# Splitting the first layer-norm tile into two column halves, and loading from two queues at the start of a gated linear-attention and token-MLP kernel

## The chip, the cores and the metric

The kernel runs on one core of a Trainium2 chip. The core has a matrix engine (TensorE, PE in the profile), a vector engine (VectorE, DVE), a scalar engine (ScalarE, ACT), a general engine (GpSimd, POOL) and a sync engine (SyncE, SP). Each works through its own list of instructions in order, and they meet through semaphores. Loads from device memory (DMA) can be issued by SP or by ACT; each of the two has a queue of its own (q1 and q10 in the profile), and the packets of both run on the core's 16 DMA engines. The metric is the device time of one execution in microseconds (us); lower is better.

## The reference, cut to what matters

```python
def _B_ref(x, w1, b1, w2, b2):
    h = _layernorm(x, axis=-1)                       # (x - mean) / sqrt(var + eps), per row of 512
    u = jnp.einsum("bsd,sf->bdf", h, w1) + b1        # contracts the 2048 tokens
    u = _gelu(u)
    y = jnp.einsum("bdf,fs->bds", u, w2) + b2
    return transpose(y)

g = _sigmoid((x * gate_w).sum(-1, keepdims=True))
a = _A_ref(x, wqkv, wo)                              # linear attention, 32 heads
out = g * a + (1 - g) * _B_ref(x, w1, b1, w2, b2)    # x: 1 x 2048 x 512, F = 1792
```

The change touches only the beginning of `_B_ref`: the layer norm of x, the first product with `w1`, and how the biases `b1` and `b2` get from rows to columns.

## The kernel before, in words

x has 2048 rows, held as 16 tiles of 128 partitions by 512 columns (`xr[:, t, :]`). F = 1792 is 14 blocks of 128 columns; the first 7 blocks (`NFA`) are half A, loaded as `w1A`, one load of 128 x 896 for each token tile t.

The start goes through these steps for each tile t. SP loads `xr` tile t and `w1A` tile t, in the order x 0, x 1, w 0, x 2, w 1, x 3, w 2, x 4, w 3 and so on. DVE takes the statistics (`ln_bn`, line 202; `ln_aggr`, line 205). ACT takes the square root (`ln_root`, line 209). DVE takes the reciprocal and writes the normalised tile `xh[:, t, :]` (`ln_apply`, lines 215 and 218). TensorE then multiplies: for tiles 0 to 11 it runs seven matmuls for each tile, one into each of seven PSUM banks `accA[j]` (`mlp1`, line 273, through the helper `mm`, so line 76 in the profile); the last four tiles (`TAIL`) are run bank by bank, with a GELU on ACT after each bank.

Two orders matter. First, DVE runs the statistics of tile t+1 before it applies tile t (line 230 before line 231), and DVE works in order. Second, nearly everything is pinned to the written order (`pin`, `keep_in_program_order`), so what stands first in the text stands first in its engine's list. In the built program each load also waits for an earlier one: eight completion semaphores are used in turn, so a load is issued only when the load eight before it has landed.

Ahead of the first real matmul TensorE runs 16 matmuls of 128 x 256 on constant data (`warm_ps`, lines 191 to 193) and one small matmul, `vps` (line 195): it turns the 30 rows `b_rows` (b1 as 14 rows and b2 as 16 rows of 128) into 30 columns. ACT copies these columns to `b1_sb` and `b2_sb` (lines 238 and 239) after the square root of tile 1. ACT issues the two small loads of `b_rows` as its first work, ahead of the load of its function table (line 140).

After half A the kernel goes on with the keys (`kacc`), the state (`Gps`), half B of the MLP (`accB`), the queries (`qacc`) and the second MLP product (`yps`), which ends it. None of these is edited.

Of the kernel before, what the change touches and what calls it, by code (L numbers as in the profile page):

```python
# [9 lines left out]
ALU = mybir.AluOpType  # L10
AX = mybir.AxisListType
BF16 = mybir.dt.bfloat16
FP32 = mybir.dt.float32
# [3 lines left out]
def kernel(  # L17
# [13 lines left out]
    nc = tc.nc  # L31
    P = nc.NUM_PARTITIONS
# [7 lines left out]
    S, D = X.shape  # L40
    F = B_w1.shape[1]
    NT = S // P
    ND = D // P
    NF = F // P
# [3 lines left out]
    NFA = NF // 2  # L48
    FA = NFA * P
    TAIL = 4  # L50

    x_view = X.rearrange("(t p) d -> p t d", p=P)
# [3 lines left out]
    w1_view = B_w1.rearrange("(t p) f -> p t f", p=P)  # L56
    w2_view = B_w2.rearrange("(f p) s -> p f s", p=P)
    b1_view = B_b1.rearrange("(f p) -> f p", p=P)
    b2_view = B_b2.rearrange("(t p) -> t p", p=P)
# [4 lines left out]
    work = ctx.enter_context(tc.tile_pool(name="work", bufs=3))  # L64
# [3 lines left out]
    def ptile(shape, dt, name):  # L68
        return persist.tile(shape, dt, name=name, tag=name)

    def bank(name):
        return psum.tile([P, SC], FP32, name=name, tag="bank")

    def mm(o, lhsT, rhs, start, stop, **kw):
        tc.keep_in_program_order(
            nc.tensor.matmul(o, lhsT=lhsT, rhs=rhs, start=start, stop=stop, **kw)  # L76
        )

    xr = ptile([P, NT, D], BF16, "xr")
    xh = ptile([P, NT, D], BF16, "xh")  # L80
# [13 lines left out]
    ident = ptile([P, P], BF16, "ident")  # L94
    gw_b = ptile([P, D], BF16, "gw_b")
    b_rows = ptile([NF + NT, P], BF16, "b_rows")
    b1_sb = ptile([P, NF], FP32, "b1_sb")
    b2_sb = ptile([P, NT], FP32, "b2_sb")
    mv = ptile([P, NT, nc.vector.BN_AGGR_DIM], FP32, "mv")
    sd = ptile([P, NT], FP32, "sd")  # L100
    rstd = ptile([P, NT], FP32, "rstd")
# [20 lines left out]
    w1A = wpool.tile([P, NT, FA], BF16, name="w1A", tag="w")  # L122
    w1B = wpool.tile([P, NT, FA], BF16, name="w1B", tag="w")

    pin = tc.keep_in_program_order

    def load(o, i, eng=None, **kw):
        pin((eng or nc.sync).dma_start(out=o, in_=i, **kw))

    def load_x(t0, t1):  # L130
        load(xr[:, t0:t1, :], x_view[:, t0:t1, :])

    def load_w1a(t):
        load(w1A[:, t, :], w1_view[:, t, 0:FA])


    tbl = work.tile([P, 1], FP32, name="tbl", tag="tbl", bufs=2)
    load(b_rows[0:NF, :], b1_view, nc.scalar)
    load(b_rows[NF : NF + NT, :], b2_view, nc.scalar)
    pin(nc.scalar.activation(out=tbl[:], in_=eps_t[:], func=ACT.Sqrt))  # L140

    load_x(0, 1)
    for t in range(5):
        load_x(t + 1, t + 2)
        load_w1a(t)
    load_w1a(5)
    for t0 in range(6, NT, 2):
        load_x(t0, t0 + 2)
        load_w1a(t0)
        load_w1a(t0 + 1)  # L150
# [9 lines left out]
    for t0 in range(0, NT, 4):  # L160
# [9 lines left out]
        out=mask[:], in_=mask[:], compare_op=ALU.is_gt, fill=1.0,  # L170
# [3 lines left out]
        out=mask[:], in_=mask[:], compare_op=ALU.is_ge, fill=0.0,  # L174
# [4 lines left out]
        out=maskH[:], in_=maskH[:], compare_op=ALU.is_gt, fill=1.0,  # L179
# [3 lines left out]
        out=maskH[:], in_=maskH[:], compare_op=ALU.is_ge, fill=0.0,  # L183
# [7 lines left out]
    warm_ps = bank("warm_ps")  # L191
    for _ in range(16):
        mm(warm_ps[:, :256], warm[:, 0:P], warm[:], True, True)
    vps = bank("vps")
    mm(vps[:, : NF + NT], b_rows[:], ident[0 : NF + NT, 0 : NF + NT], True, True)


    stats = {}

    def ln_bn(t):  # L200
        stats[t] = work.tile([P, nc.vector.BN_STATS_DIM], FP32, name="stats", tag="stats", bufs=4)
        pin(nc.vector.bn_stats(out=stats[t][:], in_=xr[:, t, :]))  # L202

    def ln_aggr(t):
        pin(nc.vector.bn_aggr(out=mv[:, t, :], in_=stats[t][:]))

    def ln_root(t0, t1):
        pin(
            nc.scalar.activation(
                out=sd[:, t0:t1], in_=mv[:, t0:t1, 1], func=ACT.Sqrt, bias=eps_t[:], scale=1.0  # L210
            )
        )

    def ln_apply(t0, t1):
        pin(nc.vector.reciprocal(out=rstd[:, t0:t1], in_=sd[:, t0:t1]))
        for t in range(t0, t1):
            pin(
                nc.vector.tensor_scalar(
                    out=xh[:, t, :], in0=xr[:, t, :],
                    scalar1=mv[:, t, 0:1], scalar2=rstd[:, t : t + 1],  # L220
                    op0=ALU.subtract, op1=ALU.mult,
                )
            )

    ln_groups = [(t, t + 1) for t in range(6)] + [(t, t + 2) for t in range(6, NT, 2)]
    ln_bn(0)
    ln_aggr(0)
    ln_root(0, 1)
    for (p0, p1), (t0, t1) in zip(ln_groups[:-1], ln_groups[1:]):
        ln_bn(t0)  # L230
        ln_apply(p0, p1)
        ln_aggr(t0)
        for t in range(t0 + 1, t1):
            ln_bn(t)
            ln_aggr(t)
        ln_root(t0, t1)
        if t0 == 1:
            pin(nc.scalar.copy(out=b1_sb[:], in_=vps[:, :NF]))
            pin(nc.scalar.copy(out=b2_sb[:], in_=vps[:, NF : NF + NT]))
    ln_apply(*ln_groups[-1])  # L240


# [26 lines left out]

    accA = [bank("accA") for _ in range(NFA)]  # L270

    def mlp1(acc, w, col, t, last):
        mm(acc[:], w[:, t, col : col + P], xh[:, t, :], t == 0, last)

    for t in range(NT - TAIL):
        for j in range(NFA):
            mlp1(accA[j], w1A, j * P, t, False)
    for j in range(NFA):
        for t in range(NT - TAIL, NT):
            mlp1(accA[j], w1A, j * P, t, t == NT - 1)  # L280
        gelu(accA[j], j)
# [59 lines left out]
    def mlp1_block(j):  # L341
        acc = bank("accB")
        for t in range(NT):
            mlp1(acc, w1B, (j - NFA) * P, t, t == NT - 1)
        return acc
# [76 lines left out]
    for b in range(NFA):  # L422
        acc = mlp1_block(NFA + b)
# [56 lines left out]
    for c in range(NSC):  # L480
        for j in range(ND):
# [5 lines left out]
                    out=pqT[:, j, c * SC : (c + 1) * SC],  # L487
                    in0=pqT[:, j, c * SC : (c + 1) * SC], in1=rex[:], op=ALU.mult,
# [55 lines left out]
```

## Time and profile before

| what | time |
|---|---|
| median of 3 runs | 165.81 us (165.55 to 165.82) |
| the profiled execution | 165.61 us |
| its span, first to last instruction | 163.9 us |
| TensorE busy in it | 158.7 us (97%) |
| DVE busy | 95.3 us (58%) |
| ACT busy | 52.1 us (32%) |
| first warming matmul | 1.25 us after the span's start |
| first `accA` matmul | 5.01 us after the span's start |

The span runs from the first to the last instruction, so the profiled execution has 1.7 us outside it. Lines of the timeline give the start, the time to the end of the group, the engine, the source line, the operation with its output and inputs, the count, and, in brackets, how long the engine stood idle before and what ended that. SPq and ACTq are the instructions with which SP and ACT issue loads. PEld is the load of a matmul's fixed operand. Lines of a table by windows give, for each stretch, the busy time and the instructions started on PE, PEld, DVE, ACT and POOL, the granted TensorE clock, the busy share of the DMA engines and what they moved in GB/s.

### The profile page before, as it was taken

The numbers are of one execution on the slowest core, as the hardware profiler recorded it, in microseconds if no ns is written. First come the engines' busy times: TensorE is split into PE (matmuls) and PEld (weight loads), VectorE is DVE, ScalarE is ACT, GpSimd is POOL, SyncE is SP. The second block draws the span as 40 slices with busy tenths as digits, with TensorE's granted clock in tenths as the row PEclk, the third lists the DMA queues.
The fourth block names the chain that finished last, engine by engine and source line by source line (L and its number), as shares of the span: only waits on it lengthen the run. The fifth ranks groups of instructions, "written<-read, shape, count | busy, mean of one in ns | idle before, by whom it ended". The sixth has DMA issues, their size and how long they took to land.

```text
span 163.9 us, 2114 instructions
## 1 busy us (share of the span) xinstructions
PE 158.7 (97%) x765; PEld 74.2 (45%) x779; DVE 95.3 (58%) x224; ACT 52.1 (32%) x87; POOL 2.0 (1%) x15
## 2 busy tenths in 40 slices
PE   6999999999999999999999999999999999999992
PEld 4444444444444455444444344444444444444461
DVE  3789989699989978482749743657205111111131
ACT  4221147952433214252348511007222221111110
POOL 4000000000000000000000000000000000000000
PEclk9999999999999999999999999999999999999999
DMA  4999996454999998000000003569982001101001
GB/s 122 293 361 374 365 147 141 101 109 86 366 384 359 367 386 305 4 4 0 2 0 0 4 32 125 187 199 301 388 322 84 32 34 48 46 32 36 32 32 32
DMA packets 26086, 25.57 MB, mean 156 GB/s; under 512 B 9820, under 2 KB 22492, under 8 KB 26076
## 3 DMA queue, kind: packets, MB, share of 16 engines
q1 hardware_dynamic: 26016, 25.43, 49.7%
q8 instruction: 6, 0.10, 0.2%
q14 instruction: 4, 0.03, 0.1%
q10 hardware_dynamic: 60, 0.01, 0.0%
HBM read 21.11 MB, written 2.23 MB: 142 GB/s over the span
## 4 chain that ended last, share of the span: by engine, by line
PE 97%; issue 1%; DVE 0%
PE yps L76 29%; PE accA L76 15%; PE accB L76 15%; PE kacc L76 8%; PE aps L76 8%; PE qacc L76 8%; PE Gps L76 8%; PE warm_ps L76 2%; PE denps L76 1%; PE kvps L76 1%; PE w2ps L76 1%; DVE ot L473 0%; DVE warm L118 0%; PE zcol_ps L76 0%; PE vps L76 0%
## 5 line engine op out<-in xcount | busy, mean ns | idle before, releaser
L76 PE MATMUL yps<-uT,w2h 128*128 128x512 bf16 (+1 forms) x234 | 50.1, 367 | 0.2
L76 PEld LDWEIGHTS <-w2h 128*128 128x128 bf16 x238 | 23.3, 98 | 25.3
L473 DVE SCALAR_TENSOR_TENSOR ot<-yps,c,ga 128x512 bf16<-128x512 f32 (+1 forms) x17 | 12.0, 717 | 36.6 <-PE yps L76 27.7
L464 ACT ACTIVATE ga<-aps,c,gg 128x512 f32<-128x512 f32 x16 | 12.4, 777 | 46.7 <-PE aps L76 46.3
L76 PE MATMUL accB<-xh,w1B 128*128 128x512 bf16 x110 | 25.1, 379 | 0.1
L76 PE MATMUL accA<-xh,w1A 128*128 128x512 bf16 x110 | 24.7, 385 | 0.1
L76 PEld LDWEIGHTS <-w1A 128*128 128x128 bf16 x112 | 11.0, 99 | 13.5 <-issue 0.8
L76 PEld LDWEIGHTS <-w1B 128*128 128x128 bf16 x112 | 10.9, 98 | 13.4 <-issue 0.4
L76 PE MATMUL kacc<-wk_sb,xT 128*128 128x512 bf16 x63 | 15.7, 379 | 0.1
L76 PE MATMUL aps<-W2sb,pqT 128*128 128x512 bf16 x63 | 15.6, 379 | 0.1
L76 PE MATMUL Gps<-pk,xr 128*128 128x512 bf16 x62 | 15.5, 379 | 0.1
L286 ACT ACTIVATE e<-qacc 128x512 bf16<-128x512 f32 x16 | 9.6, 597 | 16.1 <-PE qacc L76 15.3
L76 PE MATMUL qacc<-xT,wq_sb 128*128 128x512 bf16 x62 | 14.4, 379 | 0.1
L288 DVE TENSOR_SCALAR e<-e 128x512 bf16<-128x512 bf16 x32 | 9.2, 288 | 8.5 <-ACT e L286 8.2
L286 ACT ACTIVATE e<-kacc 128x512 bf16<-128x512 f32 x16 | 9.2, 598 | 12.7 <-DVE pk L293 6.8
L202 DVE BATCH_NORM_STATS2 stats<-xr 128x6 f32<-128x512 bf16 x16 | 10.7, 669 | 3.0 <-DMA xr<-in_A_x_dram 3.0
L293 DVE SCALAR_TENSOR_TENSOR pk<-kacc,e 128x512 bf16<-128x512 f32 x16 | 11.1, 692 | 1.0
L293 DVE SCALAR_TENSOR_TENSOR pqT<-qacc,e 128x512 bf16<-128x512 f32 x16 | 11.1, 691 | 0.6
L486 DVE TENSOR_TENSOR pqT<-pqT,rex 128x512 bf16<-128x512 bf16 x16 | 6.8, 426 | 6.1 <-DMA rex<-rd_dram 6.0
L250 DVE CUSTOM_DVE_ANT_0 junk<-xr,gw_b 128x512 bf16<-128x512 bf16 x16 | 9.9, 684 | 0.0
L76 PEld LDWEIGHTS <-xr 128*128 128x128 bf16 x64 | 6.2, 98 | 7.6
L76 PEld LDWEIGHTS <-pqT 128*128 128x128 bf16 x64 | 6.3, 98 | 7.6
(65 smaller groups left out, 80.2 us busy)
## 6 DMA issues: line engine op xcount, KB each, us to landing
w2h<-in_B_w_dram SPq DMA_DIRECT2D x4, 1792.0 KB
w1A<-in_B_w_dram SPq DMA_DIRECT2D x16, 224.0 KB
w1B<-in_B_w_dram SPq DMA_DIRECT2D x4, 896.0 KB
rex<-rd_dram SPq DMA_DIRECT2D x16, 128.0 KB
out_dram<-ot SPq DMA_DIRECT2D x15, 128.0 KB
xr<-in_A_x_dram SPq DMA_DIRECT2D x5, 256.0 KB
xr<-in_A_x_dram SPq DMA_DIRECT2D x6, 128.0 KB
wk_sb<-in_A_wqkv_dram SPq DMA_DIRECT2D x1, 512.0 KB
```

Source lines behind the costliest of these rows:

```text
L76: nc.tensor.matmul(o, lhsT=lhsT, rhs=rhs, start=start, stop=stop, **kw)
L202: pin(nc.vector.bn_stats(out=stats[t][:], in_=xr[:, t, :]))
L250: nc.vector.tensor_tensor_reduce(out=junk[:], in0=xr[:, t, :], in1=gw_b[:], scale=1.0, scalar=0.0, op0=ALU.mult, op1=ALU.add, accum_out=gp ...
L286: pin(nc.scalar.activation(out=e[:], in_=acc[:], func=ACT.Exp))
L288: nc.vector.tensor_scalar(out=e[:], in0=e[:], scalar1=1.0, scalar2=PHI_EPS, op0=ALU.min, op1=ALU.add)
L293: nc.vector.scalar_tensor_tensor(out=o, in0=acc[:], scalar=0.0, in1=e[:], op0=ALU.max, op1=ALU.add)
L464: nc.scalar.activation(out=ga[:], in_=aps[:], func=ACT.Identity, scale=gg[:, t : t + 1], bias=c2[:, t : t + 1])
L473: nc.vector.scalar_tensor_tensor(out=ot[:, d0:d1], in0=yps[:, d0:d1], scalar=c1[:, t : t + 1], in1=ga[:, d0:d1], op0=ALU.mult, op1=ALU.add,)
L486: nc.vector.tensor_tensor(out=pqT[:, j, c * SC : (c + 1) * SC], in0=pqT[:, j, c * SC : (c + 1) * SC], in1=rex[:], op=ALU.mult,)
```

## The change

Tile 0 of x is loaded as two halves of 256 columns, the first from SP and the second from ACT. ACT also loads `w1A` tiles 0 and 1, ahead of its function table. SP goes on with x 1, x 2, x 3 and `w1A` 2, then with the two small loads of `b_rows`, then with x 4, w 3, x 5, w 4, w 5 and the rest as before.

For tile 0, DVE takes statistics of each half (two `bn_stats` whose results one `bn_aggr` joins) and normalises each half by itself. TensorE multiplies the first half with all seven blocks and then the second half: 14 matmuls of 256 columns for the seven of 512. The `vps` matmul moves from before the tile 0 matmuls to behind them, and the two copies of its result on ACT move from behind the square root of tile 1 to behind all the square roots and the GELU table load.

```diff
+    HD = D // 2
+    load(xr[:, 0, 0:HD], x_view[:, 0, 0:HD])
+    load(xr[:, 0, HD:D], x_view[:, 0, HD:D], nc.scalar)
+    load_w1a(0, nc.scalar)
+    load_w1a(1, nc.scalar)
     tbl = work.tile([P, 1], FP32, name="tbl", tag="tbl", bufs=2)
-    load(b_rows[0:NF, :], b1_view, nc.scalar)
-    load(b_rows[NF : NF + NT, :], b2_view, nc.scalar)
     pin(nc.scalar.activation(out=tbl[:], in_=eps_t[:], func=ACT.Sqrt))
-
-    load_x(0, 1)
-    for t in range(5):
-        load_x(t + 1, t + 2)
-        load_w1a(t)
+    for t in range(1, 4):
+        load_x(t, t + 1)
+    load_w1a(2)
+    load(b_rows[0:NF, :], b1_view)
+    load(b_rows[NF : NF + NT, :], b2_view)
+    for t in range(4, 6):
+        load_x(t, t + 1)
+        load_w1a(t - 1)
     load_w1a(5)
...
-    vps = bank("vps")
-    mm(vps[:, : NF + NT], b_rows[:], ident[0 : NF + NT, 0 : NF + NT], True, True)
...
+    def parts(t):
+        return [(0, HD), (HD, D)] if t == 0 else [(0, D)]
+
     def ln_bn(t):
-        stats[t] = work.tile([P, nc.vector.BN_STATS_DIM], FP32, name="stats", tag="stats", bufs=4)
-        pin(nc.vector.bn_stats(out=stats[t][:], in_=xr[:, t, :]))
+        n = len(parts(t))
+        stats[t] = work.tile([P, n, nc.vector.BN_STATS_DIM], FP32, name="stats", tag="stats", bufs=4)
+        for i, (d0, d1) in enumerate(parts(t)):
+            pin(nc.vector.bn_stats(out=stats[t][:, i, :], in_=xr[:, t, d0:d1]))
...
         for t in range(t0, t1):
-            pin(
-                nc.vector.tensor_scalar(
-                    out=xh[:, t, :], in0=xr[:, t, :],
-                    scalar1=mv[:, t, 0:1], scalar2=rstd[:, t : t + 1],
-                    op0=ALU.subtract, op1=ALU.mult,
+            for d0, d1 in parts(t):
+                pin(
+                    nc.vector.tensor_scalar(
+                        out=xh[:, t, d0:d1], in0=xr[:, t, d0:d1],
+                        scalar1=mv[:, t, 0:1], scalar2=rstd[:, t : t + 1],
+                        op0=ALU.subtract, op1=ALU.mult,
+                    )
                 )
-            )
...
-        if t0 == 1:
-            pin(nc.scalar.copy(out=b1_sb[:], in_=vps[:, :NF]))
-            pin(nc.scalar.copy(out=b2_sb[:], in_=vps[:, NF : NF + NT]))
...
-    def mlp1(acc, w, col, t, last):
-        mm(acc[:], w[:, t, col : col + P], xh[:, t, :], t == 0, last)
+    def mlp1(acc, w, col, t, last, d0=0, d1=D):
+        mm(acc[:, d0:d1], w[:, t, col : col + P], xh[:, t, d0:d1], t == 0 and d0 == 0, last)
 
     for t in range(NT - TAIL):
-        for j in range(NFA):
-            mlp1(accA[j], w1A, j * P, t, False)
+        for d0, d1 in parts(t):
+            for j in range(NFA):
+                mlp1(accA[j], w1A, j * P, t, False, d0, d1)
+        if t == 0:
+            vps = bank("vps")
+            mm(vps[:, : NF + NT], b_rows[:], ident[0 : NF + NT, 0 : NF + NT], True, True)
+            pin(nc.scalar.copy(out=b1_sb[:], in_=vps[:, :NF]))
+            pin(nc.scalar.copy(out=b2_sb[:], in_=vps[:, NF : NF + NT]))
```

## The prediction

> **What bounds the kernel now.** I read the chain of waits first, then the timeline of the first 9 us, then the load queue of SP and the windows by microsecond.
>
> The chain of waits up to 13 us (start, length, what):
>
> ```profile
> 1.25 3.59 PE warm_ps L76 x16
> 4.85 0.13 PE vps L76
> 4.98 0.04 issue
> 5.01 7.59 PE accA L76 x32
> 12.60 0.05 issue
> ```
>
> From 1.25 us to the end it is TensorE without a real pause (97% of the span). So the time is when `accA` starts, plus its work, plus whatever idle time a change opens. Beyond the start there is nothing to win: 16 warming matmuls, a gap, and then a full engine.
>
> The timeline of that start:
>
> ```profile
> 2.97 0.69 DVE L202 BATCH_NORM_STATS2 stats<-xr 128x6 f32<-128x512 bf16 x1 [1.76 <-DMA xr<-in_A_x_dram]
> 3.69 0.18 DVE L205 BATCH_NORM_AGGREGATE mv<-stats 128x2 f32<-128x6 f32 x1
> 3.79 0.66 DVE L202 BATCH_NORM_STATS2 stats<-xr 128x6 f32<-128x512 bf16 x1
> 3.91 0.29 ACT L209 ACTIVATE sd<-mv,eps_t 128x1 f32<-128x1 f32 x1 [0.57 <-DVE mv L205]
> 4.37 0.14 DVE L215 RECIPROCAL rstd<-sd 128x1 f32<-128x1 f32 x1
> 4.55 0.41 DVE L218 TENSOR_SCALAR xh<-xr,mv,rstd 128x512 bf16<-128x512 bf16 x1
> 4.98 0.14 PEld L76 LDWEIGHTS <-w1A 128*128 128x128 bf16 x2
> 5.40 0.15 PEld L76 LDWEIGHTS <-w1A 128*128 128x128 bf16 x1 [0.28 <-issue]
> 5.82 0.15 PEld L76 LDWEIGHTS <-w1A 128*128 128x128 bf16 x1 [0.28 <-issue]
> 6.18 2.90 PEld L76 LDWEIGHTS <-w1A 128*128 128x128 bf16 x14 [0.21 <-issue]
> ```
>
> `xh` of tile 0 is ready at 4.55 + 0.41 = 4.96, and `accA` starts at 5.01. The weight loads come 0.42 us apart, and from 6.18 on 0.21 apart (14 in 2.90): until about 6.1 us the array runs at half its later rate, whatever the granted clock of 1.00 in the rows. The 16 warming matmuls show the same half rate: 256 columns every 0.21 us, so they stream until 1.25 + 16 x 0.213 = 4.66.
>
> Loads of SP, and the windows (PE, PEld, DVE, ACT, POOL, clock, DMA share, GB/s):
>
> ```profile
> 3.62 0.43 SPq L128 DMA_DIRECT2D w1A<-in_B_w_dram  x1
> 7.80 0.33 SPq L128 DMA_DIRECT2D w1A<-in_B_w_dram  x1
> ...
> 2.00:3.00 1.00, 1.00 (x7) 0.67 (x6) 0.03 (x1) 1.00 (x1) 0.64 (x5) 1.00 0.83 261
> 3.00:4.00 1.00, 1.00 (x6) 0.67 (x5) 0.97 (x3) 0.42 (x3) 0.00 (x0) 1.00 0.79 186
> 4.00:5.00 1.00, 0.98 (x5) 0.41 (x4) 0.96 (x4) 0.20 (x1) 0.00 (x0) 1.00 0.90 304
> ```
>
> Every load waits for the one eight before it. The issue at 7.80 (w 7) stands on w 2, which was issued at 3.62: SP was free 0.26 us earlier (7.21 + 0.33 = 7.54), so w 2 landed near 7.78. By then x 0 to x 3 and w 0 to w 2 had to be in, 4 x 131 + 3 x 229 = 1,212 KB. The row of 3 to 4 us shows a dip, 186 against 304 GB/s.
>
> **The change part by part.**
>
> *Start of tile 0.* A half of `bn_stats` isn't in the trace. Its cost lies between half of 0.66 (0.33) and the whole (0.69); with a fixed part like the reciprocal's 0.14 it is 0.14 + 0.26 = 0.40, so the two take 0.8, some 0.1 more than the one. A half apply is likewise 0.14 + (0.41 - 0.14)/2 = 0.28, which lets TensorE begin 0.13 earlier. If the data come as before, the first half of `xh` is ready near 4.55 + 0.28 = 4.83. Without the small matmul and wait at 4.77 to 4.98, `accA` could start between 4.70 (end of the warming) and 5.01; I take 4.87. The gain of 0.14 lies in the slow stretch before 6.1 and is worth half, 0.07 us. The most it can be is (5.01 - 4.70)/2 = 0.16.
>
> *Matmuls of tile 0.* 14 of 256 columns for seven of 512: the last tile of the kernel runs 28 such in 3.07 us of the chain (0.11 each) against 0.216 for 512, so 7 x 0.004 = 0.03 us at most. `vps` behind them costs one weight load that nothing covers, 0.10, plus a few columns: 0.1 to 0.2 (its row today is 0.13, and hidden in the wait for `xh`); I take 0.15.
>
> *Tile 1 of x against `w1A` 0.* In order on DVE, statistics of tile 1 stand before the reciprocal of tile 0. Today x 1 comes before w 0; now w 0 goes out on ACT's queue beside it. If x 1 lands as before (by 3.79), nothing moves; if it must share with w 0's 229 KB at 304 GB/s, up to 0.75 us later, 4.5, which pushes `accA` to about 5.7 and costs 0.35 us. I take x 1 at 4.0 and `accA` at about 5.1, which takes back the 0.07 and no more.
>
> *ACT.* Three issues in place of two, at SP's 0.47 apart until 2.2 (at the 0.66 of ACT's longer one, 2.8); then the table load 1.28 and 0.2: ready at 3.7 to 4.3 for the root that runs at 3.91 now. The cover is the 0.66 of statistics of tile 1, until 4.45: hidden, or up to 0.2 late. The two copies land between the table's end at 24.38 and the first GELU at 24.79, 0.41 us in which ACT idles; they need about 0.2. Hidden.
>
> *SP.* x 2, x 3 and w 2 go out at 1.73, 2.20 and 2.67 in place of 2.20, 3.15 and 3.62; the bias loads take the places at 3.15 and 3.62; x 4 stays near 4.1. Slots: the two small loads hold two of eight, so x 6 waits for w 2 instead of w 1 and goes out some 1 us later than its 6.60. It landed at 11.26 (DVE waits for it there), 4.7 us after its issue, so it is queueing that sets its landing, and I cost this at nothing. If that cover is gone, tile 6 is late: its `xh` is ready at 14.39 and wanted at 14.63, a slack of 0.24.
>
> *The bias loads and `vps`.* This is the step that decides. Today `b_rows` goes first, on a queue of its own, and is long there at 4.77. Now it stands on SP's queue behind x 0 to x 3 and w 2, and `vps` stands on TensorE between tile 0 and tile 1. So TensorE can't go on to tile 1 before w 2 and the rows behind it are through, though tile 1 needs neither. When is that? Bytes ahead are the same 1,212 KB that landed at 7.78. The earlier issue fills the dip: 304 - 186 = 118 KB between 3 and 4 us, and about as much less again around 2.75, at 300 GB/s together 0.4 to 0.5 us. Two halves mean 128 packets more, at the 0.83 x 16 / 332 = 40 ns of a packet in the row of 2 to 3 us up to 0.3 us over 16 engines; I take half. So the biases land near 7.78 - 0.5 + 0.15 = 7.45, between 6.2 (1,212 KB at 345 GB/s from 2.2, plus 0.5 of landing) and 7.9. Tile 0 ends at 5.01 + 0.56 + 7 x 0.216 = 7.08 (0.56 being half of the slow stretch to 6.1), little moved by the start. TensorE waits 7.45 - 7.08 = 0.37, then `vps` 0.15: tile 1 starts 0.52 late.
>
> The sum replaces the start's gain: once it waits here, a start earlier by a tenth is lost in the wait. Nothing takes 0.5 us back, since TensorE is full until the end. The profiled execution, 165.61, becomes 166.13; it lies 0.2 below the median of 165.81, which would give 166.33. I forecast 166.2 us.
>
> The Trainium skill bears on this in "DMA: Bandwidth & Descriptors", section "Issuing engines are not separate DMA queues": loads issued from several engines share the same 16 DMA engines, so the second issuer saves only issue time. By it the bytes in front of the biases come no faster than one queue's, which would leave the landing at 7.78 and the time near 166.5; the dip in the row of 3 to 4 us speaks for some gain from issue time.
>
> **The rivals.** A change within 0.2% (0.33 us) is about what a measurement of this kernel can't tell from none.
>
> 1. *The biases come in time*, before 7.1. For: 345 GB/s is reached at 7 us, and at this rate they are there at 6.2. Against: w 2 landed at 7.78. The start's 0.07 to 0.16 is set against 0.15 for `vps` and 0.03: 165.55 to 165.8, the same.
> 2. *Slower half of the start*: x 1 shares with w 0, and `accA` starts at 5.7. If the biases are in time it is 165.61 + 0.35 + 0.15 = 166.1; if not, the wait swallows it. For: DVE's order. Against: the second queue starts no sooner than SP's.
> 3. *Faster*: the array's change of rate follows TensorE's busy time and not the clock on the wall. The gap from 4.66 to 5.0 closes, the rate changes 0.3 us sooner, and the whole 0.3 us counts, not half: 165.61 - 0.31 = 165.3, and over the 0.2% only if `vps` costs nothing. It decides if `accA` starts by 4.7 and the biases are there by 6.8. Against: DVE can't have `xh` before 4.8, and the wait on the biases.
>
> For rival 3 the Trainium skill has a rule in "TensorE: Matmul & The Clock Gate", Part 1: the window of 3413 ns that decides on the rate runs freely and isn't reset by the kernel. By that rule the change of rate stays near 6.1; the one switch in this trace can't tell the two apart.
>
> **How the numbers follow.** The wait for the biases over 0.33 us net, alone or with a late x 1: 0.50. Rival 2 with its own price just over the bound, or a late tile 6: 0.06. In time, or a wait too short to count: 0.35. Rival 3: 0.09. So slower 0.56, same 0.35, faster 0.09. The range: biases at 7.9 with `vps` and a slow second queue give about +1.0 on the profiled execution and +0.2 for its place, 166.9; the low end takes in rival 1 at 165.6. The likeliest case alone is 165.9 to 166.9.
>
> **What would show it.** TensorE idle behind the 256-column matmuls of `accA`, ended by a load of `b_rows`, at 6.9 to 7.5; `accA` starting between 4.8 and 5.2; DVE's statistics of tile 1 waiting for x 1; x 2 and x 3 landing before their 5.33 and 7.21; no idle TensorE after 8 us. It would be wrong if `vps` runs at once behind tile 0, or if the rate changes at another moment than 6.1.

## The result and the profile after

The changed kernel takes 166.32 us in the median against 165.87 us for the kernel before, 22 runs each; the ratio is 1.0030 with a 95% interval of 1.0016 to 1.0045. So it is 0.3% slower, as forecast (166.2 us, slower). The ratios here leave out executions more than 1.5% above a kernel's fastest one, the medians don't, so where some executions lie near 168 us the two can differ.

Two executions of the changed kernel were profiled, 166.66 us (span 164.9) and, in the last comparison, 166.31 us (span 164.6). The first one's start, in the timeline:

```profile
3.11 0.75 DVE L211 BATCH_NORM_STATS2 stats<-xr 128x6 f32<-128x256 bf16 x2 [1.91 <-DMA xr<-in_A_x_dram]
4.18 0.69 DVE L211 BATCH_NORM_STATS2 stats<-xr 128x6 f32<-128x512 bf16 x1
4.58 0.10 PEld L76 LDWEIGHTS <-w1A 128*128 128x128 bf16 x1 [0.21 <-DMA w1A<-in_B_w_dram]
4.98 0.60 DVE L228 TENSOR_SCALAR xh<-xr,mv,rstd 128x256 bf16<-128x256 bf16 x2
5.38 1.47 PEld L76 LDWEIGHTS <-w1A 128*128 128x128 bf16 x13 [0.70 <-issue]
7.06 0.09 PEld L76 LDWEIGHTS <-b_rows 30*128 30x128 bf16 x1 [0.21 <-issue]
7.18 2.27 PEld L76 LDWEIGHTS <-w1A 128*128 128x128 bf16 x12
```

`accA` starts at 5.38, not at 5.01 and not at the 4.87 to 5.1 of the forecast. The load of `b_rows` at 7.06 follows tile 0 without a wait on a DMA: the wait that the forecast rests on isn't there. The 13 weight loads in 1.47 us, 0.11 for 256 columns, are at the full rate: here the array's rate changed near 5.5, not 6.1. That is luck for this execution: tile 1 starts at 7.18, only 0.10 later than the 7.08 of before. Not all of the late start is x 1's: the first statistics start at 3.11, 0.14 later than before, because the halves of x 0 come later in this execution, and x 1 adds about 0.16 (the statistics of tile 1 follow 1.07 behind those of tile 0, against 0.91 in the run below that has only the halves).

What this execution loses comes later, where DVE waits for tiles 6 and 7 of x (one load), and TensorE for DVE (timelines of DVE and PE):

```profile
12.48 0.69 DVE L211 BATCH_NORM_STATS2 stats<-xr 128x6 f32<-128x512 bf16 x1 [2.10 <-DMA xr<-in_A_x_dram]
...
13.74 1.67 PE L76 MATMUL accA<-xh,w1A 128*128 128x512 bf16 x7 [0.34 <-DVE xh L228]
15.72 2.53 PE L76 MATMUL accA<-xh,w1A 128*128 128x512 bf16 x11 [0.30 <-DVE xh L228]
```

Tile 5 would start at 7.18 + 4 x 7 x 0.216 = 13.23 and starts at 13.74; tile 6 would start at 7.18 + 5 x 7 x 0.216 = 14.74 and starts at 15.72. That is 1.0 us, the difference of the spans. The second profiled execution loses at another place. Its start:

```profile
4.65 0.69 DVE L211 BATCH_NORM_STATS2 stats<-xr 128x6 f32<-128x512 bf16 x1 [0.65 <-DMA xr<-in_A_x_dram]
5.84 1.69 PE L76 MATMUL accA<-xh,w1A 128*128 128x256 bf16 x14 [0.99 <-DVE xh L228]
7.46 0.18 PE L76 MATMUL vps<-ident,b_rows 30*128 30x30 bf16 x1
7.58 10.72 PE L76 MATMUL accA<-xh,w1A 128*128 128x512 bf16 x47
```

DVE stands idle for x 1, the normalisation of tile 0 stands behind it, and TensorE idles 0.99 us until 5.84. Tile 1 starts 0.50 later than before; at tile 6 another 0.2 us is lost (there the weight loads stop for 0.31 us, ahead of 15.34, where 0.11 is usual). Together that is the 0.7 us by which the span is longer. One profile would have given the wrong cause, in either case.

Why x 1 is late shows in the DMA queues of the first execution, between 2 and 3 us and then between 3 and 4 us (packets, MB, share of 16 engines; q1 is SP's, q10 is ACT's):

```profile
q1 hardware_dynamic: 164, 0.10, 38.6%
q10 hardware_dynamic: 140, 0.07, 27.5%
...
q10 hardware_dynamic: 124, 0.21, 55.5%
q1 hardware_dynamic: 120, 0.11, 37.2%
```

Between 2 and 3 us SP's queue, which carries the first half of x 0 and then x 1, moves 0.10 MB; before the change it moved 0.25 MB in the same microsecond. Between 3 and 4 us the two queues move about one packet each in turn, 124 to 120 (131 to 102 in the second execution), but a packet of `w1A` carries 1.8 KB and one of x 1 KB. So x, which DVE waits for, gets half the bytes of `w1A`. "DMA: Bandwidth & Descriptors" of the Trainium skill, section "Queues, rings and completion order", says that each DMA engine goes round the queues packet by packet; the counts agree, at 124 to 120, though the order of single packets isn't in this view.

### The profile page after: what moved, and what is told of

Same layout as the page of the kernel before. It is cut to its first block, busy times and chain, and to the rows that moved or that the text cites. A ratio compares the mean times of both kernels' runs of the same rounds, so it can differ in the third digit from the quotient of the medians.

```text
span 164.9 us, 2145 instructions
## 1 busy us (share of the span) xinstructions
PE 159.4 (97%) x786; PEld 74.9 (45%) x786; DVE 95.3 (58%) x226; ACT 52.0 (32%) x87; POOL 2.0 (1%) x15
## 4 chain that ended last, share of the span: by engine, by line
PE 89%; DMA 6%; DVE 2%; SPq 1%; issue 0%
PE yps L76 29%; PE accB L76 15%; PE accA L76 9%; PE qacc L76 8%; PE Gps L76 8%; PE kacc L76 8%; PE aps L76 8%; DMA xr<-in_A_x_dram 6%; SPq L128 1%; DVE stats L211 1%; PE denps L76 1%; PE kvps L76 1%; PE w2ps L76 1%; DVE xh L228 1%; DVE ot L486 0%
## 5 line engine op out<-in xcount | busy, mean ns | idle before, releaser
L76 PE MATMUL accA<-xh,w1A 128*128 128x512 bf16 (+1 forms) x119 | 24.9, 367 | 1.2 <-DVE xh L228 1.2
L76 PEld LDWEIGHTS <-w1A 128*128 128x128 bf16 x119 | 11.6, 98 | 14.3 <-issue 1.9
L211 DVE BATCH_NORM_STATS2 stats<-xr 128x6 f32<-128x512 bf16 (+1 forms) x17 | 10.7, 636 | 4.1 <-DMA xr<-in_A_x_dram 4.0
L76 PEld LDWEIGHTS <-xT 128*128 128x128 bf16 x64 | 6.3, 98 | 7.5
```

What stands on the lines that cost most here:

```text
L211: pin(nc.vector.bn_stats(out=stats[t][:, i, :], in_=xr[:, t, d0:d1]))
```

## The experiments

Four theories stood against each other. A: the small bias loads take SP's time and two of eight load slots, x 6/7 comes late, TensorE waits at tiles 5 and 6. B: the halves cost DVE and the start. C, the forecast: TensorE waits for the biases behind tile 0. D: x 1, sharing with `w1A` 0 and 1, is late and DVE's order passes that on to tile 0. Each ratio is to runs of the kernel before on the same chip. The first four ran on one chip, the next four on a second, the last four on a third.

**Bias loads at the end of half A's loads** (the changed kernel, edited)

```diff
-    load(b_rows[0:NF, :], b1_view)
-    load(b_rows[NF : NF + NT, :], b2_view)
...
+    load(b_rows[0:NF, :], b1_view)
+    load(b_rows[NF : NF + NT, :], b2_view)
     load(gw_b[:], gw_row_view.to_broadcast([P, D]))
...
-        if t == 0:
+        if t == NT - TAIL - 1:
             vps = bank("vps")
```

> Theory A (the two small bias loads take SP's time and two of the eight load slots in the first 4 us, so that the loads behind them go out late, x 6/7 lands after 12 us and TensorE waits for tiles 5 and 6): with the bias loads behind all loads of half A and the bias matmul behind tile 11, x 4 goes out before 4.2 us, x 6/7 lands by 11.4, TensorE doesn't wait at tiles 5 and 6, and the time falls to within 0.15 us of the kernel before. Theory B (the later start of tile 0, 5.38 instead of 5.01, is what costs): the start stays at 5.3 to 5.4 and the time stays 0.3 to 0.5 us above the kernel before. Theory C (TensorE waits for the bias loads behind tile 0, as forecast): the time falls by the wait at that place, of which the profile of the changed kernel shows none, so nothing changes.

Measured: median 167.94 us, eight of eleven executions at 167.71 and above, the other three 165.48 to 165.94; ratio 1.0055 (1.0016 to 1.0094). No theory expected this. The profiled execution (168.63 us), timelines of DVE and of the weight loads:

```profile
5.36 0.69 DVE L211 BATCH_NORM_STATS2 stats<-xr 128x6 f32<-128x512 bf16 x1 [1.41 <-DMA xr<-in_A_x_dram]
...
6.55 3.09 PEld L76 LDWEIGHTS <-w1A 128*128 128x128 bf16 x15 [0.90 <-issue]
9.92 0.15 PEld L76 LDWEIGHTS <-w1A 128*128 128x128 bf16 x1 [0.28 <-issue]
10.33 0.75 PEld L76 LDWEIGHTS <-w1A 128*128 128x128 bf16 x4 [0.27 <-issue]
```

x 1 is there at 5.36, `accA` starts at 6.55, and then the array runs at half rate (0.21 for 256 columns, later 0.41 for 512) until about 10.3. Start plus half of the slow stretch is 6.55 + 1.9 = 8.4, against 5.01 + 0.56 = 5.57 before: 2.9 us, and the span is 3.0 longer. This is where D was formed, with a second half: the idle time ahead of `accA` puts off the change of rate.

**Tile 5 normalised ahead of the statistics of tile 6** (the changed kernel, edited)

```diff
+        if t0 == 6:
+            ln_apply(p0, p1)
         ln_bn(t0)
-        ln_apply(p0, p1)
+        if not (t0 == 6):
+            ln_apply(p0, p1)
```

> The changed kernel with one swap: tile 5 is normalised ahead of the statistics of tile 6. Theory A: x 6/7 still lands late, 12 to 12.5 us, but tile 5 no longer waits for it; of the 1.0 us that tiles 5 and 6 lose in the profile of the changed kernel at most 0.3 is left, and the median falls by 0.2 to 0.4 us to about the kernel before. Theories B and C: no change, 0.3 to 0.5 us above the kernel before.

Measured: 166.65 us, ratio 1.0061 (1.0034 to 1.0088). Taking the coupling away at tile 5 gains nothing. The profile shows D again: DVE waits 0.87 us for x 1 and `accA` starts at 5.93. That doesn't rule out A, because the same coupling is there once more, one group later (timeline of DVE):

```profile
14.15 0.69 DVE L211 BATCH_NORM_STATS2 stats<-xr 128x6 f32<-128x512 bf16 x1 [0.62 <-DMA xr<-in_A_x_dram]
```

These are the statistics of tile 8, and the normalisation of tile 6 stands behind them. So a late x 8/9 holds tile 6, and no run here takes that apart.

**Only the bias loads and their matmul moved** (the kernel before, edited)

```diff
-    load(b_rows[0:NF, :], b1_view, nc.scalar)
-    load(b_rows[NF : NF + NT, :], b2_view, nc.scalar)
...
         load_w1a(t)
+        if t == 2:
+            load(b_rows[0:NF, :], b1_view)
+            load(b_rows[NF : NF + NT, :], b2_view)
```

and `vps` with its copies behind tile 0, as in the change.

> The kernel before with one part of the change: the bias loads go from ACT's queue to SP's behind w1A 2, and the bias matmul behind tile 0. Theory A: x 4 and all loads behind it go out 0.4 to 0.9 us later, x 6/7 lands at 12 or later, TensorE waits at tiles 5 and 6, and the kernel is 0.3 to 0.9 us slower than before. Theory B: same as before within 0.15 us. Theory C: TensorE waits behind tile 0 for the biases, which land near 7.9 here: 0.7 to 0.9 us slower, with no wait at tiles 5 and 6.

Measured: 166.78 us, ratio 1.0075 (1.0051 to 1.0100). This is C, with its wait where it was put; tile 1 starts at 7.93, 0.85 later than before, within the 0.7 to 0.9 expected (timeline of PE):

```profile
5.01 1.67 PE L76 MATMUL accA<-xh,w1A 128*128 128x512 bf16 x7 [0.16 <-DVE xh L217]
7.81 0.18 PE L76 MATMUL vps<-ident,b_rows 30*128 30x30 bf16 x1 [1.13 <-DMA b_rows<-in_B_b_dram]
```

So the forecast's mechanism is real; in the two profiles of the changed kernel it is out of sight, because the biases are there by the time tile 0 ends.

**Only the halves in the computation** (the kernel before, with the change's `parts`, `ln_bn`, `ln_apply` and `mlp1`; loads, `vps` and copies as before)

```diff
+    def parts(t):
+        return [(0, HD), (HD, D)] if t == 0 else [(0, D)]
...
-        for j in range(NFA):
-            mlp1(accA[j], w1A, j * P, t, False)
+        for d0, d1 in parts(t):
+            for j in range(NFA):
+                mlp1(accA[j], w1A, j * P, t, False, d0, d1)
```

> The kernel before with the other part alone: tile 0 of x is loaded whole as before, but its statistics, normalisation and matmuls go in two halves. Theory A: no cost, within 0.1 us of before; the start is near 4.9 to 5.0. Theory B: it costs what the halves cost DVE, the start is at 5.1 or later, 0.1 to 0.4 us slower. Theory C: within 0.1 us of before.

Measured: 165.92 us, ratio 1.0001 (0.9989 to 1.0014). B falls: the halves alone neither cost nor gain. `accA` starts at 5.08; the two half statistics take 0.75 us against 0.69 for the whole, the join 0.21 against 0.18, and the first half's normalisation 0.35 on the chain against 0.41.

**Tile 0 normalised ahead of the statistics of tile 1** (the changed kernel, edited)

```diff
+        if t0 == 1:
+            ln_apply(p0, p1)
         ln_bn(t0)
-        ln_apply(p0, p1)
+        if not (t0 == 1):
+            ln_apply(p0, p1)
```

> The changed kernel with one swap on DVE: tile 0 is normalised ahead of the statistics of tile 1. Theory D (x 1 shares the DMA engines with w1A 0 and 1 from ACT's queue, lands at 4 to 5.4 us, and DVE, in order, holds tile 0 behind it; when the start comes after about 6.3 the array also stays at half rate to about 10 us): accA starts at 4.8 to 5.1 in the profile, or when w1A 0 lands, if that is later; runs of 167.6 us and more vanish or become rare; the median is 165.8 to 166.2. Theory A (late x 6/7 at tiles 5 and 6): no change, median 166.3 to 166.7 with some runs near 168. Theory C (the bias loads): the wait moves behind tile 0, vps starts at 7.1 to 7.6 with TensorE idle up to 0.6 us before it.

Measured: 166.13 us, ratio 1.0012 (0.9992 to 1.0032), slowest execution 166.96. With x 1 off the path, `w1A` 0 is next in line (weight loads):

```profile
5.07 2.10 PEld L76 LDWEIGHTS <-w1A 128*128 128x128 bf16 x14 [0.70 <-DMA w1A<-in_B_w_dram]
```

The chain of waits begins with this load: 3.80 us from its issue at 1.23. As D expects, one swap on DVE with no load touched brings the start back to 5.08 and a median near that of before. How much of the loss it takes away this run can't say, because the changed kernel didn't run on this chip and the interval overlaps that of the result. The profiled execution (166.68) still loses 0.42 at tile 1 and 0.67 at tile 6, which starts at 15.72, behind the late statistics of tile 8.

**`w1A` 0 and 1 back on SP's queue** (the changed kernel, edited)

```diff
-    load_w1a(0, nc.scalar)
-    load_w1a(1, nc.scalar)
...
     for t in range(1, 4):
         load_x(t, t + 1)
-    load_w1a(2)
+        load_w1a(t - 1)
```

> The changed kernel with w1A 0 and 1 back on SP's queue in the order of before; ACT loads only the second half of x 0. Theory D: x 1 lands by 3.9, accA starts at 4.9 to 5.1, no run near 168; then the bias loads stand behind one queue as in the forecast, land near 7.8, and TensorE waits 0.7 to 1.1 us for them: 166.4 to 166.9. Theory A: x 4 and later go out late, TensorE waits at tiles 5 and 6, 166.3 to 166.9 with runs near 168 as often as in the changed kernel.

Measured: 166.89 us, ratio 1.0070 (1.0050 to 1.0089). As D expects, x 1 is in time (DVE takes it at 3.95 without a wait) and `accA` starts at 5.14; and then C is back:

```profile
8.13 0.17 PE L76 MATMUL vps<-ident,b_rows 30*128 30x30 bf16 x1 [1.30 <-DMA b_rows<-in_B_b_dram]
```

**24 warming matmuls for 16** (the changed kernel, edited)

```diff
-    for _ in range(16):
+    for _ in range(24):
```

> The changed kernel with 24 warming matmuls in place of 16, so that TensorE is busy until x 1 is there. If the idle time before accA is what keeps the array at half rate in the runs near 168, these runs vanish, at the price of at most 0.5 us where the start would have been earlier: all runs between 165.7 and 166.8, median 165.9 to 166.4. If the runs near 168 come from late loads, as many stay as in the changed kernel (3 of 22).

Measured: 166.60 us, ratio 1.0044 (1.0028 to 1.0061), six runs from 166.29 to 167.12. None is near 168, but six runs could miss what 3 of 22 showed, and the price is higher than expected. The kernel before had three of its own on this chip, 167.24, 167.69 and 168.04 among 23, and nothing here explains those. The profile is worth more. The warming matmuls' weight loads come 0.11 apart from 4.27 on, so here the rate changed at about 4.2. Tile 1 starts at 7.07, as before the change, and tile 6 at 15.35 in place of 14.63: with the late start made good, the whole 0.7 us of this execution is A, with DVE waiting 1.77 us for x 6/7.

**Swaps and `w1A` 0 on ACT behind the biases** (the kernel before, edited)

```diff
     load(b_rows[NF : NF + NT, :], b2_view, nc.scalar)
+    load(w1A[:, 0, :], w1_view[:, 0, 0:FA], nc.scalar)
...
-        load_w1a(t)
+        if t > 0:
+            load_w1a(t)
```

with the swap on DVE for `t0 in (1, 6)`.

> The kernel before, with the bias loads first on ACT's queue as before, w1A 0 as the third load on ACT's queue, and tiles 0 and 5 normalised ahead of the next tile's statistics; no halves. Theory D: with DVE's order swapped a late x 1 no longer holds tile 0; accA starts at 4.85 to 4.95, x 2 and later go out 0.47 us earlier: 0.05 to 0.3 us faster than before. Theory A: the same, since no slots are held. If w1A 0 lands after 5.0 it is the start instead, and the kernel is the same as before or up to 0.2 us slower.

Measured: median 165.97 us, ratio 1.0037 (0.9996 to 1.0077). Seven executions lie between 165.65 and 166.00, four between 167.46 and 168.15, and one at 963.55, which nothing here explains. In the profiled one (165.65) `accA` starts at 5.05, the moment `w1A` 0 lands. That the four near 168 are those where it lands much later would fit; it isn't shown, and the kernel before has executions near 168 on this chip too.

**The changed kernel once more**

> The changed kernel once more, unedited, on the chip of this comparison. Theory D (x 1 lands late and DVE's order holds tile 0 behind it): accA starts between 5.2 and 6.6 with DVE waiting for x 1, or for w1A 0, and the time follows the start: its median is 0.3 to 0.8 us above the kernel before, and some runs are at 167.6 us and more. Theory A: accA starts near 5.3 and what is lost is at tiles 5 and 6.

Measured: 166.84 us, ratio 1.0059 (1.0032 to 1.0086), from 165.86 to 167.97, four of twelve at 167.47 and above. Its profile, shown above, is D with little of A.

**Both swaps in the changed kernel** (`t0 in (1, 6)`)

> The changed kernel with both swaps on DVE: tile 0 is normalised ahead of the statistics of tile 1, tile 5 ahead of those of tile 6. Theory D with A beside it: the start is at 4.8 to 5.1 and tile 5 no longer waits for x 6/7; the median is 0.1 us below to 0.15 us above the kernel before, with no run at 167.6 or more. If the one swap at tile 0 did all there was to do, this is no faster than with that swap alone, 0.12% above before.

Measured: 166.39 us, ratio 1.0025 (1.0008 to 1.0042), slowest 166.94: 0.45 us below the changed kernel on the same chip, and still slower than before. What is next in line shows in its profile:

```profile
4.91 1.91 PE L76 MATMUL accA<-xh,w1A 128*128 128x256 bf16 x14
7.26 0.17 PE L76 MATMUL vps<-ident,b_rows 30*128 30x30 bf16 x1 [0.44 <-DMA b_rows<-in_B_b_dram]
15.54 2.75 PE L76 MATMUL accA<-xh,w1A 128*128 128x512 bf16 x12 [0.44 <-DVE xh L228]
```

With the start at 4.91 the wait for the biases comes out, 0.44 us, with the biases there at 7.23; then a late load of x costs as much again: DVE takes tile 8 only at 14.27, and the normalisation of tile 6 stands behind it. My expectation of 0.1 below to 0.15 above before was too good.

**The swaps alone** (the kernel before, `t0 in (1, 6)`)

> The kernel before with the same two swaps and nothing else. Its x 1 comes first on one queue, so there is little to free: accA starts at 4.87 to 4.95 in place of 5.01, which counts half, and tiles 5 and 6 had no wait: 0 to 0.15 us faster, the same within what can be measured.

Measured: 165.91 us, ratio 1.0000 (0.9986 to 1.0014). `accA` starts at 4.92, but tile 6 then waits 0.26 us for DVE, which had waited 0.26 us for tile 8 of x. No version here beats the kernel before.

**Late biases with 24 warming matmuls** (the first experiment's kernel, with the 24)

```diff
-    for _ in range(16):
+    for _ in range(24):
```

> The kernel with the late bias loads, which had 8 of 11 runs at 167.7 us and more, with 24 warming matmuls in place of 16. If the array stays at half rate there because TensorE stands idle for 1 to 2 us ahead of accA, the idle time is filled, the rate changes before 8.1 us, and no run is above 167.4; the median is 166.0 to 166.9. If those runs come from late loads alone, as many stay near 168.

Measured: 166.28 us, ratio 1.0024 (1.0005 to 1.0043), all twelve between 165.81 and 167.06, where eight of eleven had been at 167.71 and above. x 1 is late here too (DVE waits 0.99 us for it, until 4.80), but TensorE has no gap, and the executions near 168 are gone, on a chip where the changed kernel has four of twelve. Together with the slow stretch in the first one's profile this points to the idle time. It stops short of proof, because the kernel with 16 warming matmuls and late biases didn't run on this chip.

## Why the prediction was right or wrong

The direction and the size were right: 166.2 forecast, 166.32 measured, in the range of 165.6 to 166.9. The mechanism was not the one I put first, so the number is in part luck: the wait that was to cost 0.37 us cost nothing in either profile of the changed kernel, and other waits of a like size stood in its place. Step by step:

- *The bias loads and `vps`*: the step that was to decide failed. I had the biases landing at 7.45 and TensorE waiting 0.37 us. In both profiles of the changed kernel they were there by 7.06 and 7.46, and `vps` ran behind tile 0 without a wait. In the first, tile 0 ended as forecast (7.06 against 7.08), and it was the landing that was wrong: the biases came at least 0.39 us before 7.45, which is the condition of my rival 1. From 3 to 6 us the core took in 317, 377 and 352 GB/s with two queues, against 186, 304 and 239 before, so the second queue brought bytes in sooner. In the second, tile 0 ended at 7.46, past any wait. The wait showed where tile 0 ended before the biases came: 0.44 us with the biases there at 7.23, and 1.13 and 1.30 us with `w1A` on SP's queue, which put them at 7.80 and 8.10. So the other landing in the prediction, 7.78 because a second issuer saves only issue time, is off by 0.55 us and more. One step of the sum is also put badly: "about as much less again around 2.75" would make 0.8 us of the two dips, and next to no wait. The window from 2.75 to 3 us, at 152 GB/s against 300, lacks 37 KB, and with that the 0.5 us comes out.
- *Tile 1 of x against `w1A` 0*: the term that was mis-sized, and the largest loss where x 1 was very late. I bounded x 1 at 4.5 and took 4.0, with `accA` at 5.1. DVE had it at 4.18, 4.65, 4.74 and 5.36 in four profiles with `w1A` 0 and 1 on ACT's queue, 16 warming matmuls and DVE's order as in the change, and `accA` started at 5.38, 5.84, 5.93 and 6.55. (With 24 warming matmuls DVE had it at 4.14 and 4.80.) The bound left out two things. Between 3 and 4 us the queues share by packets and not by bytes. And in the microsecond from 2 to 3 us the core took in 131 to 193 GB/s in these four against 261 before. With the halves on two queues but `w1A` on SP's it was 248, in one profile, so the halves alone don't do it. How `w1A` on ACT's queue does isn't shown: in that microsecond ACT's queue moved mostly the second half of x 0 (0.07 MB in 140 packets). The next microsecond took in more than before, so it is the order of the loads that is lost and not the bytes. This was my rival 2, to which I gave 0.06 together with a late tile 6.
- *SP's slots*: costed at nothing, wrong. With the bias loads in SP's stream DVE has x 6/7 at 11.7 to 12.6 us in seven profiles where it waits for it; without them at 11.20, 11.26 and 11.31 in three. The later issue that I worked out isn't what does it: x 6/7 went out at 6.85 and 7.12 in the two executions of the changed kernel, 0.25 and 0.52 later than its 6.60 and not 1 us. The two slots do hold back x 4, which went out at 4.55 and 4.83 for 4.10. It stands on `w1A` 0, eight loads before it, and went out just as that landed (4.58 and 4.85 in the weight loads). After x 6/7 is issued the core takes in less: 238 and 218 GB/s from 8 to 10 us of the first execution, against 362 and 326 before. Why is not shown. It cost 1.0 us in one execution of the changed kernel and 0.2 us in the other, where the late start covered the rest; the swap at tile 5 alone did not move the median, but tile 6 also stands behind x 8/9.
- *Matmuls and statistics in halves*: right, a cost of nothing (1.0001). The earlier start that the half apply was to bring did not come either: 5.08 with the halves alone, against 5.01.
- *Rival 3*, a rate that follows TensorE's busy time and changes sooner when a gap closes: it falls in this form. TensorE's first matmul is at 1.25 us in every profile shown, and the rate changed at about 4.2, 5.5, 6.1 and 10.3. Busy time does count in another way, because the last of these follows a long gap. My assumption that the change stays near 6.1 was wrong as well: the moment differs from execution to execution, and the freely running window on which I rested it is no reason for a fixed moment. With the start at 5.38, a change at 5.5 in place of 6.1 is worth 0.3 us.

So the loss is three waits, one behind the other on TensorE: for x 1 through DVE, for the biases, for x 6/7 or x 8/9 through DVE. The first to be long covers the others, and the one that shows differs from execution to execution. Which share of the median belongs to which is not settled; the two swaps together took 0.0034 off the ratio on one chip (1.0059 to 1.0025, with intervals that just overlap), and the rest is what still stands behind it.

## What to carry to other kernels

A second issuing queue does more than save issue time: it changes which of the first loads lands first, and a queue with larger packets takes more of the bytes. Look for the engine that works in order, and ask what its next step waits for, before moving a load off the queue that kept that order. When one wait is forecast behind a start that may itself slip, work out both; the earlier wait hides the later one, and removing it brings the later one out.

## What the runs showed of the hardware

TensorE's rate changes from half to full at a moment that isn't tied to the kernel's start: near 4.2, 5.5 and 6.1 us in three profiles whose first matmul is at 1.25 us each time. When TensorE stood idle from 4.85 to 6.55 the change came only at about 10.3: 3.75 us at half rate, which cost 1.9 us. With the gap filled by eight more matmuls none of twelve executions, on another chip, was near 168 us (the slowest 167.06). "TensorE: Matmul & The Clock Gate" of the Trainium skill, Part 1, has a freely running window of 3413 ns that must have been busy; the spread of the moments agrees with it, and so does the change after the gap, 3.75 us after the matmuls resumed, which leaves room for one whole window.
